# Sparse attention and token mixing on one core: value loads behind the product that frees their place, second pair's keys on ACT's queue, one turned tile, later tables, another spread of the decoding

## The chip, the cores and the metric

The kernel runs as one program on one core of a Trainium2 chip. The metric is the device time of the whole program in microseconds, from the program's start to its end; lower is better.

## The reference

Block-sparse attention over 4 batches x 8 heads x 768 positions x 64, followed by a token and channel mixer. Cut to what matters:

```
q, k, v: (4, 8, 768, 64) f32; 24 blocks of 32 positions; sampled_blocks: (24, 3) int64
mask[block i, block j] = |i-j| <= 1, or i or j in {0, 23}, or j in sampled_blocks[i]
attn = softmax(where(mask, q k^T / 8, -1e9));  x = (attn v) as (4, 768, 512)
theta = x @ w_theta;  zr, zi = x cos(theta), x sin(theta)
u = x + w_tok_r zr + w_tok_i zi   (over positions);  out = u + relu(u @ w_ch)
```

The four `moe` weights reach the device as 64-bit words, and the kernel decodes them into a high and a low part.

## The kernel before

**Units.** Two batches at a time form a pair `bp` (0 or 1). In each pair the program first does 8 *wide* units (`b`, `e`, `z`: query blocks 0 and 23 against all 768 keys), then 22 *sparse* units, one for each query block `i` from 1 to 22: that block of 32 queries for 16 heads against 8 key blocks (three of the window, block 0, block 23 and three sampled ones). All 60 units stand in the list `units`, so number 8 is the first sparse unit of the first pair and 30 the first wide one of the second.

**The order.** `tc.manual_schedule()` keeps the instructions of each engine in the order in which `attention` writes them: nothing is reordered there. The main loop is a software pipeline over steps `n`. TensorE (PE) does in step `n` the scores `S` of unit n+1, turns (transposes) the weights of unit n, and multiplies the turned weights of unit n-1 with the values into `X`. VectorE (DVE) normalises `X` of unit n-2 into `xo` (`finish`), gathers the sampled keys of unit n+2 into `kg`, takes the row extremum `m` of unit n+1's scores, and does some decoding of weights. ScalarE (ACT) copies the other keys into `kg`, does its part of the decoding, copies the turned weights from PSUM to SBUF, and takes the exponentials `P` of unit n+1. GpSimd (POOL) issues one indirect DMA per sparse unit, which gathers the values of the sampled blocks into `vb` (three buffers). After the attention the token mixer follows, whose order the framework's scheduler chooses; some of its first loads and transposes lie among the last sparse units.

**Loads.** All other DMAs are issued from SyncE's queue (SP), in the order of the program: a DMA that must wait holds back what stands behind it. `load_window` brings the window's values into `va`, of which there are two (`vas[i % 2]`), so that the load for a unit can start only when the product `X` two units earlier has read its buffer. In step n the loop writes first `finish` (with the store of `xo` to `xs`), then `load_window` of unit n and `gather_v` of unit n+1. The DMAs of queues in hardware share eight completion semaphores in turn, so each also waits until the DMA eight before it has landed. The keys `kb` of a pair have one buffer; those of the second pair are loaded on SP, with the first two value tiles `vw` of its wide units, three steps before the pair changes.

**Decoding.** The weights come in pieces of 128 x 512. Each piece takes three phases (`bits`, `rest`, `low`) on DVE, with `start` and `high` on ACT, and 66 phases cover 22 pieces. Before, a wide step does two phases and a sparse step one until none is left, so the last of the 60 units have none. After `low` of a piece SP loads the piece after next into `raw` (two buffers).

**Tables.** `Tables` loads `sampled_blocks` and makes, with some two dozen small DVE instructions, the block numbers and row numbers for the gathers. Before, it stands ahead of the first wide unit.

**Turning.** `transposed` turns up to four 128 x 128 pieces into a PSUM tile `T` (two buffers of one bank each); a sparse unit has two such tiles, `Ta` and `Tb`, each with a copy of 128 x 512 on ACT into `pa` and `pb`.

## Time and profile before

| | |
|---|---|
| time, median of 3 runs | 663.11 us (658.08 to 669.28) |
| the profiled execution | 654.65 us, of it 652.9 us span |
| mean granted TensorE clock | 0.952 |
| busy share of the span | PE 86%, DVE 71%, ACT 55%, POOL 7% |
| wide units of the first pair end near | 46 us |
| sparse units, first pair | 46 to 168 us |
| wide units of the second pair | 164 to 204 us |
| sparse units, second pair | 204 to 310 us |
| token mixer | from 288 us (first loads) to the end |

The profile is of one execution. Its rows name an engine, a line of the kernel, `out<-in`, and in brackets the idle time before an instruction with what ended it; `SPq` is the issue of a DMA on SP's queue, not the transfer. A table by stretches gives, for each stretch in us from the span's start, its length, each engine's busy time with the number of instructions, the granted clock, the share of time that the 16 DMA engines are busy, and their rate.

### The profile page before, as it was taken

The page shows a single profiled execution, that of the slowest core. Times are in us where ns is not written, and L with a number is a line of the kernel's source. Part 1 is how long each engine was busy: PE and PEld are TensorE (multiplying, and loading weights), DVE is VectorE, ACT ScalarE, POOL GpSimd, SP SyncE. Part 2 cuts the span into 40 slices and gives each one's busy share as a digit, 9 for nine tenths or more (in the row PEclk, how much of TensorE's full clock was granted, in tenths as well). Part 3 has the DMA queues.
Part 4 walks back from the last instruction along what each step waited for, and adds up shares of the span by engine and source line. Part 5 has one row for each costly group of instructions (what it writes and reads, how often), then busy time and mean ns, then how long its engine had stood idle before and what let it go on. Part 6 is the DMA issues. An engine that isn't in the chain of part 4 may idle for free.

```text
span 652.9 us, 19231 instructions
## 1 busy us (share of the span) xinstructions
PE 563.3 (86%) x7808; PEld 482.2 (74%) x7808; DVE 465.5 (71%) x1239; ACT 362.2 (55%) x834; POOL 43.5 (7%) x56
## 2 busy tenths in 40 slices
PE   4967777773977877867989999999999999999997
PEld 1545555552544655546889999999999999999997
DVE  4497798781799877845898988575783856846654
ACT  1576776771487766755656655345553456433530
POOL 1101121210100222210000000000000000000000
PEclk9997898896799988995999999999999999999999
DMA  8757889899479897776542233221142111221102
GB/s 305 229 163 201 236 247 261 237 261 326 130 233 234 231 241 215 209 208 168 144 136 81 61 83 115 93 69 49 46 134 88 63 50 43 69 67 60 33 1 96
DMA packets 79960, 96.53 MB, mean 148 GB/s; under 512 B 5312, under 2 KB 64832, under 8 KB 79488
## 3 DMA queue, kind: packets, MB, share of 16 engines
q1 hardware_dynamic: 74944, 77.73, 40.1%
q0 software_dynamic: 4928, 17.57, 10.2%
q8 instruction: 61, 1.00, 0.7%
q14 instruction: 27, 0.22, 0.1%
HBM read 82.70 MB, written 12.58 MB: 146 GB/s over the span
## 4 chain that ended last, share of the span: by engine, by line
PE 57%; DMA 22%; DVE 12%; ACT 3%; issue 3%; SPq 2%; DVEq 1%; ACTq 0%
DMA va<-in_vr_dram 14%; PE y L560 8%; PE y L561 8%; PE y L562 8%; PE X L316 5%; PE S L285 4%; PE o L583 3%; PE o L584 3%; PE o L585 3%; DMA raw_ch<-in_w_ch_dram 3%; PE h L524 3%; PE h L523 2%; PE h L522 2%; DMA xr<-xs 2%; PE Ta L303 2%
## 5 line engine op out<-in xcount | busy, mean ns | idle before, releaser
L316 PE MATMUL X<-va,pa 128*32 128x65 f32 (+1 forms) x1408 | 50.8, 239 | 45.1 <-DMA va<-in_vr_dram 41.5
L297 ACT ACTIVATE P<-S,m 128x256 f32<-128x256 f32 x176 | 69.0, 477 | 22.5 <-DVE m L288 22.4
L316 PEld LDWEIGHTS X<-va,pa 128*32 128x32 f32 (+1 forms) x1408 | 36.4, 119 | 54.8 <-DMA va<-in_vr_dram 31.9
L560 PE MATMUL y<-w_tok_r_hi,zh 128*128 128x384 f32 x192 | 64.7, 338 | 3.9 <-ACT zh L547 3.8
L288 DVE TENSOR_REDUCE m<-S 128x2 f32<-128x512 f32 x88 | 56.6, 685 | 14.2 <-PE S L285 6.8
L561 PE MATMUL y<-w_tok_r_lo,zh 128*128 128x384 f32 x192 | 64.3, 335 | 0.0
L561 PE MATMUL y<-w_tok_i_lo,zh 128*128 128x384 f32 x192 | 64.2, 334 | 0.0
L560 PE MATMUL y<-w_tok_i_hi,zh 128*128 128x384 f32 x192 | 64.1, 334 | 0.0
L562 PE MATMUL y<-w_tok_r_hi,zl 128*128 128x384 f32 x192 | 63.3, 335 | 0.0
L285 PE MATMUL S<-kg,q 64*32 64x256 f32 x1408 | 56.0, 418 | 6.8 <-issue 4.0
L562 PE MATMUL y<-w_tok_i_hi,zl 128*128 128x384 f32 x192 | 61.0, 334 | 0.0
L267 POOL DMA_INDIRECT vb<-in_vr_dram,rows x44 | 42.0, 955 | 246.5 <-PE X L316 232.6
L522 PE MATMUL h<-w_theta_hi,xTh 128*128 128x256 f32 x192 | 54.6, 285 | 0.1
L524 PE MATMUL h<-w_theta_hi,xTl 128*128 128x256 f32 x192 | 54.5, 284 | 0.0
L523 PE MATMUL h<-w_theta_lo,xTh 128*128 128x256 f32 x192 | 54.4, 283 | 0.0
L316 PE MATMUL X<-vb,pb 128*32 128x65 f32 (+1 forms) x1408 | 50.4, 237 | 0.2 <-issue 0.2
L303 PEld LDWEIGHTS Ta<-ident,P 128*128 128x128 f32 x176 | 21.3, 149 | 35.9 <-ACT P L297 22.5
L311 ACT COPY pa<-Ta 128x512 f32<-128x512 f32 x44 | 26.1, 592 | 36.4 <-PE Ta L303 36.2
L533 ACT ACTIVATE cs<-rr 128x256 f32<-128x256 f32 x48 | 19.8, 415 | 47.4 <-DVE rr L531 47.4
L303 PE MATMUL Ta<-ident,P 128*128 128x128 f32 x176 | 37.3, 314 | 9.4 <-ACT P L297 6.1
L526 ACT ACTIVATE t<-h,up_int 128x256 f32<-128x256 f32 x48 | 22.6, 472 | 39.2 <-PE h L524 32.8
L583 PE MATMUL o<-uh,w_ch_hi 128*128 128x384 f32 x128 | 42.5, 336 | 1.1 <-DVE of L589 0.9
(128 smaller groups left out, 1413.8 us busy)
## 6 DMA issues: line engine op xcount, KB each, us to landing
xa<-xs SPq DMA_DIRECT2D x192, 64.0 KB
va<-in_vr_dram SPq DMA_DIRECT2D x30, 260.0 KB
vw<-in_vr_dram SPq DMA_DIRECT2D x8, 780.0 KB
xr<-xs SPq DMA_DIRECT2D x24, 256.0 KB
out_dram<-of SPq DMA_DIRECT2D x32, 192.0 KB
q<-in_qT_dram SPq DMA_DIRECT2D x22, 256.0 KB
xs<-xo SPq DMA_DIRECT2D x44, 128.0 KB
kb<-in_kT_dram SPq DMA_DIRECT2D x3, 1536.0 KB
```

The source lines that it names most:

```text
L285: nc.tensor.matmul(sc[32 * p : 32 * p + 32, e, b, :], q[rows, b, p, :], kg[rows, :, 4 * b + p, :], start=True, stop=True)
L288: nc.vector.tensor_reduce(m[:, e], sc[:, e], axis=AX.X, op=ALU.min)
L297: nc.scalar.activation(pt[:, e, b, :], sc[:, e, b, :], AF.Exp, bias=m[:, e, b : b + 1], scale=-1.0)
L303: nc.tensor.transpose(t[:, k, :], pt, ident)
L316: nc.tensor.matmul(x[32 * p : 32 * p + 32, g, :], pt[0:rows, k, 32 * p : 32 * p + 32], v[0:rows, v0 + 65 * p : v0 + 65 * p + 65], start=st ...
L522: nc.tensor.matmul(ps, hi[:, c, :], wh[:, c, :], start=c == 0, stop=False)
L523: nc.tensor.matmul(ps, hi[:, c, :], wl[:, c, :], start=False, stop=False)
L524: nc.tensor.matmul(ps, lo[:, c, :], wh[:, c, :], start=False, stop=c == 3)
L560: nc.tensor.matmul(acc, zh[:, dd], wh[:, j, tt], start=j == 0 and m == 0, stop=False)
L561: nc.tensor.matmul(acc, zh[:, dd], wl[:, j, tt], start=False, stop=False)
L562: nc.tensor.matmul(acc, zl[:, dd], wh[:, j, tt], start=False, stop=j == 5 and m == 1)
L583: nc.tensor.matmul(ps, wh[:, c, :], uh, start=c == 0, stop=False)
```

## The change

Six things, all inside `attention`, `Tables` and the loop:

1. `load_window` moves from the start of step n (unit n, behind `finish`) to the end of the step before it (unit n+1, right behind `values` of unit n-1, the product that reads its buffer last). `gather_v` moves in the same way, to unit n+2.
2. In the second pair `kb` (two loads) and the first two `vw` are issued from ACT's queue, after the exponentials of step 27.
3. A unit's turned weights have one tile: `T` of two banks with one buffer instead of two of one bank, filled by eight (wide: six) transposes, and one copy of 128 x 1024 (768) instead of two.
4. The decoding does one phase in each step, two in the odd steps of wide units, up to one step past the last unit. It is still 66 phases.
5. `Tables` only loads at the start (its load ahead of the keys now); its DVE work, `make`, stands behind step 0.
6. The two first loads of `q` and their exclusion in the loop are written in another way; the loads are the same.

```diff
             load_edges(0)
+            tab = Tables(nc, cp, sampled)
             turn_edges(0)
             for p in range(0, 4, 2):
                 load_k(0, 0, p, 2)
-            tab = Tables(nc, cp, sampled)
...
             for n in range(len(units) + 2):
                 phases = 0
-                if 2 <= n < len(units):
-                    phases = 2 if units[n][1] == "w" else 1
+                if 2 <= n <= len(units):
+                    phases = 1 + (n < len(units) and units[n][1] == "w" and n % 2)
                 do(n - 2, finish, finish_wide)
-                do(n, load_window)
-                do(n + 1, gather_v)
...
-                    for b in range(2):
-                        load_k(1, b)
-                        load_v_wide(1, 0, b)
                 decoder.ahead(phases)
                 do(n + 1, scores, scores_wide)
                 do(n, turn, turn_wide)
                 do(n + 1, weights, weights_wide)
+                if turns:
+                    for b in range(2):
+                        load_k(1, b, queue=nc.scalar)
+                        load_v_wide(1, 0, b, nc.scalar)
                 decoder.go(phases)
+                if n == 0:
+                    tab.make(nc, cp)
                 do(n - 1, values, values_wide)
+                do(n + 1, load_window)
+                do(n + 2, gather_v)
...
-        ps_t = ctx.enter_context(tc.tile_pool(name="ps_t", bufs=2, space=PSUM))
+        ps_t = ctx.enter_context(tc.tile_pool(name="ps_t", bufs=1, space=PSUM))
...
-        def transposed(pts, name):
-            t = ps_t.tile([P, 4, 128], F32, tag="T", name=f"T{name}")
+        def turned(pts, name):
+            n = len(pts)
+            t = ps_t.tile([P, 8, 128], F32, tag="T", name=f"T{name}")
             for k, pt in enumerate(pts):
                 nc.tensor.transpose(t[:, k, :], pt, ident)
-            return t[:, : len(pts)]
+            out = wp.tile([P, 8, 128], F32, tag="pT", name=f"pT{name}")
+            nc.scalar.copy(out[:, :n], t[:, :n])
+            return out
```

On SP's queue, in the middle of the first pair's sparse units, the order before is this (`xo_7` is the result of sparse unit i = 7; the load behind it is for i = 9):

```order
L339 DMA xs<-xo_7_1447 128x2x128
L260 DMA va_119<-in_vr_dram 64x1040
L200 DMA q_13_1452<-in_qT_dram 128x512
L59 DMA raw_tok_r_1508<-in_w_tok_r_dram 128x1024
L339 DMA xs<-xo_8_1546 128x2x128
L260 DMA va_118<-in_vr_dram 64x1040
L339 DMA xs<-xo_9_1642 128x2x128
```

The same place of the changed program:

```order
L263 DMA va_119<-in_vr_dram 64x1040
L341 DMA xs<-xo_7_1388 128x2x128
L203 DMA q_13_1391<-in_qT_dram 128x512
L59 DMA raw_tok_i_1444<-in_w_tok_i_dram 128x1024
L263 DMA va_118<-in_vr_dram 64x1040
L341 DMA xs<-xo_8_1484 128x2x128
```

Each load of `va` has moved ahead of the store of the result whose product frees the buffer; in one step of three it now stands right behind a load of `raw`.

Where the pair changes, SP's queue before has the keys between two loads of values:

```order
L260 DMA va_118<-in_vr_dram 32x1040 x2
L206 DMA kb_2528<-in_kT_dram 128x3072
L346 DMA vw_0_0_2530<-in_vr_dram 128x6x260
L206 DMA kb_2528<-in_kT_dram 128x3072
L346 DMA vw_0_1_2533<-in_vr_dram 128x6x260
L339 DMA xs<-xo_19_2613 128x2x128
L260 DMA va_119<-in_vr_dram 64x1040
```

In the changed program they stand on ACT, between the exponentials of sparse unit i = 21 and the copy of its turned weights:

```order
L300 ACTIVATE P_21_2465<-S_21_2434,m_21_2451 128x256 x4
L209 DMA kb_2470<-in_kT_dram 128x3072
L348 DMA vw_0_0_2472<-in_vr_dram 128x6x260
L209 DMA kb_2470<-in_kT_dram 128x3072
L348 DMA vw_0_1_2475<-in_vr_dram 128x6x260
L80 CAST w_tok_i_hi<-da_tok_i_2345 128x512
L309 COPY pT_21_2551<-T_21_2542 128x1024
```

The four transfers have left SP's queue, and an issuing ACT stands ahead of the next copy and exponentials.

On DVE, among the first pair's wide units, two phases stand between the extrema `mw` of one unit and the next before:

```order
L357 TENSOR_REDUCE mw_011_286<-SW_011_277 128x1
L67 TENSOR_SCALAR da_theta_275<-da_theta_275 128x512
L68 TENSOR_SCALAR da_theta_275<-da_theta_275 128x512
L69 SCALAR_TENSOR_TENSOR da_theta_275<-raw_theta_183,da_theta_275 128x512
L75 TENSOR_SCALAR ds_theta_305<-da_theta_275 128x512
L77 SCALAR_TENSOR_TENSOR raw_theta_183<-raw_theta_183,ds_theta_305 128x512
L357 TENSOR_REDUCE mw_100_346<-SW_100_337 128x1
```

and one now:

```order
L359 TENSOR_REDUCE mw_011_280<-SW_011_271 128x1
L67 TENSOR_SCALAR da_theta_269<-da_theta_269 128x512
L68 TENSOR_SCALAR da_theta_269<-da_theta_269 128x512
L69 SCALAR_TENSOR_TENSOR da_theta_269<-raw_theta_143,da_theta_269 128x512
L359 TENSOR_REDUCE mw_100_332<-SW_100_323 128x1
```

In every second wide step the phase `rest`, `low` or `bits` that stood there has moved to a later step; at the far end the last seven phases now lie among the last sparse units of the second pair and one step behind them.

## The prediction

> **What bounds the kernel now.** I read the chain that ended last first, then a table by stretches, and at last the rows in order of time. In the chain the first line is by engine, the second by line:

> ```profile
> PE 57%; DMA 22%; DVE 12%; ACT 3%; issue 3%; SPq 2%; DVEq 1%; ACTq 0%
> DMA va<-in_vr_dram 14%; PE y L560 8%; PE y L561 8%; PE y L562 8%; PE X L316 5%; PE S L285 4%; PE o L583 3%; PE o L584 3%; PE o L585 3%; DMA raw_ch<-in_w_ch_dram 3%; PE h L524 3%; PE h L523 2%; PE h L522 2%; DMA xr<-xs 2%; PE Ta L303 2%
> ```

> The loads of `va` are 14% of the chain, some 90 us; the PE lines `y`, `o`, `h` are the token mixer. Then by stretches: start, wide units, sparse units in their steady part, change of pair, wide units, sparse units, tail, mixer. The columns are the stretch, its length, busy us and instructions of PE, PE's weight loads, DVE, ACT and POOL, the granted clock, the DMA engines' busy share and GB/s:

> ```profile
> 0.00:14.50 14.50, 7.25 (x32) 1.72 (x32) 5.13 (x32) 1.49 (x2) 1.46 (x12) 1.00 0.84 299
> 14.50:46.00 31.50, 25.54 (x512) 14.98 (x512) 22.01 (x42) 19.75 (x37) 2.92 (x3) 1.00 0.70 206
> 62.50:145.60 83.10, 63.70 (x1876) 44.58 (x1876) 70.06 (x186) 62.90 (x145) 17.46 (x18) 0.94 0.90 249
> 145.60:168.00 22.40, 11.60 (x174) 6.65 (x174) 5.90 (x14) 4.40 (x10) 0.00 (x0) 0.61 0.78 266
> 168.00:204.00 36.00, 30.26 (x700) 18.11 (x698) 33.55 (x69) 26.41 (x53) 2.86 (x3) 0.96 0.71 205
> 204.00:288.00 84.00, 64.17 (x1871) 44.33 (x1871) 66.44 (x182) 60.85 (x142) 16.94 (x18) 0.94 0.82 224
> 288.00:313.00 25.00, 18.06 (x357) 15.40 (x354) 13.43 (x46) 13.30 (x29) 0.91 (x1) 0.73 0.72 183
> 313.00:653.00 340.00, 331.31 (x2066) 329.33 (x2064) 235.89 (x643) 162.36 (x397) 0.00 (x0) 1.00 0.25 75
> ```

> The mixer keeps PE 97% busy and is not touched. POOL's 18 gathers count the sparse units of a steady part: 83.10 / 18 = 4.62 us a unit in the first pair and 84.00 / 18 = 4.67 in the second, of which DVE is busy 3.89 and 3.69, PE 3.5, ACT 3.5, and the DMA engines 90% and 82%. So no engine fills a unit. The wide units from 168 to 204 are another matter: DVE is 93% busy. The change of pair, 22.4 us, is idle on all engines for more than half.

> **The loop of a sparse unit**, from the rows in order of time (start, length, engine, what; in brackets the idle time before):

> ```profile
> 89.11 1.11 SPq L260 DMA_DIRECT2D va<-in_vr_dram  x1
> 90.64 0.32 PE L316 MATMUL X<-vb,pb 128*32 128x65 f32 x8
> 91.34 0.69 DVE L84 TENSOR_TENSOR w_tok_r_lo<-da_tok_r,raw_tok_r 128x512 fp32r<-128x512 f32 x1
> 92.35 0.42 DVE L326 TENSOR_TENSOR xo<-X,sm 128x256 f32<-128x256 f32 x1
> 92.53 0.35 SPq L59 DMA_DIRECT2D raw_tok_r<-in_w_tok_r_dram  x1
> 93.46 0.54 SPq L260 DMA_DIRECT2D va<-in_vr_dram  x1
> 94.67 0.32 PE L316 MATMUL X<-va,pa 128*32 128x65 f32 x8 [1.48 <-DMA va<-in_vr_dram]
> 95.49 0.30 PE L316 MATMUL X<-vb,pb 128*32 128x65 f32 x8
> 97.65 1.85 SPq L260 DMA_DIRECT2D va<-in_vr_dram  x2
> 100.33 0.32 PE L316 MATMUL X<-va,pa 128*32 128x65 f32 x8 [2.50 <-DMA va<-in_vr_dram]
> ```

> A product ends at 90.96 and frees its buffer. The next load into it is issued only at 93.46: DVE does decoding first, then `xo`, and SP stands at the store of `xo` until then. The load is used at 100.33, 6.87 us after its issue; the one of 89.11 at 94.67, after 5.56. The product at 94.67 ends at 95.79, and the load that it frees goes out at 97.65, 1.86 us later. So two units take 1.1 (product) + 1.9 to 2.5 (to the issue) + some 6.2 (to the use) = 9.2 to 9.8; the measured 2 x 4.62 = 9.24 is this loop.

> **The change, part by part.**

> *Loads of values earlier.* In two steps of three the load now waits for the product alone: 0.1 to 0.2 us instead of 1.9. In the third it stands behind a load of `raw`, which waits for DVE's L84: that ends at 92.03 here, 1.07 us after the product, and the issue takes 0.35, so 1.4 instead of 2.5. The loop becomes 1.1 + 0.2 + 6.2 = 7.5, or 8.7 with `raw`: 3.8 to 4.4 us a unit. What is late next is DVE, 3.89 busy in an order that never packs it fully, and the DMA engines: at 90% busy they can give 10%, 4.16 a unit. Bounds: no gain if those engines are saturated already, 0.73 us a unit if DVE at 3.89 set the pace. With both limits near 4.1 and the `raw` steps above them I take 4.35, 0.27 us less, in both pairs: 2 x 18 x 0.27 = **-9.7 us**. The store of `xo`, now behind the load, has a unit's time before its buffer is wanted. The gathers do not move: POOL has nothing else in its queue.

> *Second pair's keys on ACT's queue.* The rows around the change of pair:

> ```profile
> 141.70 1.57 ACT L297 ACTIVATE P<-S,m 128x256 f32<-128x256 f32 x4 [0.61 <-DVE m L288]
> 141.81 0.51 SPq L206 DMA_DIRECT2D kb<-in_kT_dram  x1
> 144.15 5.35 SPq L339 DMA_DIRECT2D xs<-xo  x1
> 149.60 0.48 SPq L260 DMA_DIRECT2D va<-in_vr_dram  x1
> 151.09 2.79 PE L355 MATMUL SW<-kb,qe 64*32 64x512 f32 x16 [4.39 <-DMA kb<-in_kT_dram]
> 162.18 0.44 PE L316 MATMUL X<-va,pa 128*32 128x65 f32 x8 [6.41 <-DMA va<-in_vr_dram]
> ```

> Behind the four issues (two halves of `kb`, two `vw`) SP's next issue holds the queue 5.35 us, so `va` goes out at 149.60 and lands behind the keys at 162.1. Now `va` leaves before them and PE's wait of 6.41 goes; but the keys are issued behind the exponentials, at 143.3 instead of 141.8, and the scores on PE wait for them 1.5 us longer. ACT pays four issues of 0.5, which it has while PE waits. -6.4 + 1.5, and about 1 for bandwidth that `va` now takes from the keys: **-4 us**; between +0.5 (ACT itself held 5.35 us, the keys 1.5 later, less the old wait) and -6.4.

> *Decoding spread out.* The phases among the second pair's wide units, on DVE in order of time (rows between left out):

> ```profile
> 181.37 0.69 DVE L83 TENSOR_TENSOR da_tok_i<-da_tok_i,w_tok_i_hi 128x512 f32<-128x512 f32 x1
> 182.70 0.95 DVE L357 TENSOR_REDUCE mw<-SW 128x1 f32<-128x768 f32 x1
> 183.56 0.41 DVE L67 TENSOR_SCALAR da_tok_r<-da_tok_r 128x512 f32<-128x512 f32 x1
> 185.20 0.43 DVE L75 TENSOR_SCALAR ds_tok_r<-da_tok_r 128x512 int32<-128x512 int32 x1
> 186.27 0.15 DVE L323 TENSOR_SCALAR sm_w<-XW 128x4 f32<-128x4 f32 x1
> 195.77 1.29 DVE L288 TENSOR_REDUCE m<-S 128x2 f32<-128x512 f32 x2
> ```

> A phase costs 1.6 (`bits`, 183.56 to 185.20), 1.1 (`rest`, to 186.27) and 1.3 us (`low`, 181.37 to 182.70), 1.35 on average. From the extremum at 182.70 to that of the first sparse unit at 195.77 three steps take 4.4 each, and DVE paces them. Three phases leave steps 32, 34 and 36 (step 30's lies in the wait for the keys): 4.05 us, unless PE, 30.26 of 36 busy, some 3.4 a step, takes over early; -3.2. In the first pair's, three leave steps 2, 4 and 6, again 4.05 us; DVE is busy 22.01 us of 31.50 there, but what is idle lies mostly ahead of the first phases (4.51 below), so -3.6. Together **-6.8**, between -3 and -8.

> The seven phases come back in steps 54 to 60, 9.5 us of DVE work. Most lies in steps whose loop I have already priced at 4.35; in the tail, 288 to 313, DVE has 11.6 us free, but the mixer's transposes queue behind the last phases: **+1.5**, between 0 and +5.

> *Tables later.* At the start DVE makes the tables before the first extremum:

> ```profile
> 8.35 5.33 PE L355 MATMUL SW<-kb,qe 64*32 64x512 f32 x28 [0.29 <-DMA kb<-in_kT_dram]
> 9.46 0.28 DVE L125 CAST sb_given<-sb_raw 128x72 f32<-128x72 int32 x1 [5.54 <-DMA sb_raw<-in_sampled_dram]
> 14.54 1.81 DVE L357 TENSOR_REDUCE mw<-SW 128x1 f32<-128x768 f32 x2
> 16.57 1.51 PE L303 MATMUL Tw<-ident,PW 128*128 128x128 f32 x6 [2.88 <-ACT PW L364]
> 20.87 0.96 DVE L357 TENSOR_REDUCE mw<-SW 128x1 f32<-128x768 f32 x1 [4.51 <-PE SW L355]
> ```

> The tables take 5.1 us (9.46 to 14.54), and later DVE idles 4.51. Moved into that gap they are free, and PE's transposes need not wait 2.88 at 16.57; the scores of unit 1 end only at 13.7, with the smaller load ahead some 0.4 later. So **-2.2**, between 0 and -4.5.

> *One turned tile.* Copies now, by form (busy, mean ns of one, idle before):

> ```profile
> L311 ACT COPY pa<-Ta 128x512 f32<-128x512 f32 x44 | 26.1, 592 | 36.4 <-PE Ta L303 36.2
> L373 ACT COPY pw<-Tw 128x256 f32<-128x256 f32 x16 | 6.1, 380 | 0.0
> L297 ACT ACTIVATE P<-S,m 128x256 f32<-128x256 f32 x176 | 69.0, 477 | 22.5 <-DVE m L288 22.4
> ```

> From 380 for 256 columns and 592 for 512, 1024 cost an estimated 592 + 2 x 212 = 1016 instead of 2 x 592, which overlap by 0.1: even. But the copy starts only after all transposes: six take 1.51 above, so the second four about 1.0, of which the first copy's 0.59 ran beside; the turn ends some 0.45 later. `P` waits for DVE's `m` 22.4 us in all, which covers that: **0**; without the cover +0.45 a unit, 20 us over 44 units.

> Sum: -9.7 - 4 - 6.8 + 1.5 - 2.2 = -21.2. The profiled execution took 654.65 (1.75 around the span): 633.4 after. It lies 8.5 below the median of the runs, 663.11, and I carry that over: 641.9, **642 us**.

> [...]

> **The rivals.**

> *A, the DMA engines are the bound (0.22).* 0.90 busy at 249 GB/s speaks for it; against it stand 299 GB/s at 0.84 in the first stretch and 266 at 0.78 around the change of pair. Earlier loads then land no earlier, and the keys steal what `va` gains: both terms go, -21.2 + 13.7 = -7.5, 655.6.

> *B, the keys interleave with the values (0.12).* A sparse unit's other traffic is 4.62 us x 249 GB/s = 1.15 MB; taken in between, it delays the keys by 1.15 / 0.266 = 4.3 us, and PE waits as long for them as it did for `va`. The keys' term is 0: 645.9. [...]

> *C, slower: ACT's longer turn (0.06).* If, with DVE relieved, `P` starts at the copy's end and not at `m`, each sparse unit pays 0.45 and each wide one 0.3: 44 x 0.45 + 16 x 0.3 = 24.6, and the loads and the wide units gain nothing, since ACT's turn paces both: 24.6 - 4 - 2.2 + 1.5 = +19.9, 683. It decides as soon as ACT waits for transposes where it now waits for `m`; the 36.2 us before `pa` speak for it, 3.5 us busy of 4.62 against it.

> *D, the load stays late (part of the forecast's range).* If the load behind `raw` in one step of three paces the rest, the unit stays at 4.5: 6 us less gain, 648.

> **How the numbers follow.** The forecast with D has 0.60, A 0.22, B 0.12, C 0.06. A measurement of this kernel can tell about 2% from no change: 13.3 us, so 649.8 is the border. Of the forecast some 0.52 lies below it, of B 0.09, of A 0.04: faster 0.65. C gives slower 0.06, the rest 0.29. The range takes in A with a poorer tail, 660; downwards the sparse units at 4.15 (36 x 0.2 = 7.2 more) and the upper ends of wide units and start (3.5) give 631, a little more 629.

> **What would show it.** Loads of `va`: issue within 0.3 us of the product's end in two of three; the idle time before `X`, 1.48 and 2.50 above, gone in most units; DVE's share near 90% in the first pair's sparse units, 4.35 us apart. Keys: the product of unit i = 21 directly behind the first `SW`, without its 6.41. Wide units: 3.3 us a step, DVE idle in the even ones. Start: first `mw` at about 11. It is wrong if the units stay at 4.6 with DMA at 0.95, if `P` waits for copies, or if the mixer's first `y` moves less than the attention's end.

## The result and the profile after

The changed kernel takes **638.8 us** (median of 4 runs, 636.82 to 639.49) against 664.38 for the kernel before in runs beside it: ratio 0.964, 95% interval 0.957 to 0.972, faster. The forecast was 642.0, range 629 to 660. The total was right; two of its terms were not, and they are of more use than the total. Stretches below are those of one execution of each kernel; how far they move from one execution to another is shown further down.

The profiled execution took 636.82 us, its span is 635.0 (before 654.65 and 652.9). The chain that ended last, first by engine, then the head of its line by lines:

```profile
PE 66%; DMA 18%; DVE 8%; issue 4%; ACT 2%; SPq 1%; DVEq 1%; ACTq 0%
PE y L555 10%; PE y L556 10%; PE y L557 10%; DMA va<-in_vr_dram 10%; PE X L318 4%; PE S L288 4%; PE T L307 4%; PE h L519 3%; PE h L518 3%; PE o L578 3%; PE h L517 3%; PE o L580 3%; PE o L579 3%; DMA kb<-in_kT_dram 3%; PE SW L357 2%
```

`va` fell from 14% to 10%; "issue", time in which an engine waits for nothing that the profile shows, rose from 3% to 4%. By stretches (columns as in the prediction): first wide units, the 18 sparse units from X of the second to X of the twentieth, change of pair, wide units, 16 sparse units of the second pair. A DMA packet's whole time counts in the stretch in which it begins, so the share of a short stretch can come out above 1:

```profile
13.00:41.50 28.50, 27.17 (x480) 14.59 (x472) 23.06 (x61) 17.74 (x27) 2.93 (x3) 1.00 0.80 256
57.70:139.30 81.60, 64.93 (x1873) 44.00 (x1872) 69.00 (x185) 61.23 (x124) 18.89 (x18) 0.96 0.93 256
139.30:151.40 12.10, 8.38 (x175) 5.67 (x174) 5.94 (x14) 4.85 (x8) 0.00 (x0) 0.86 1.04 342
151.40:187.20 35.80, 30.19 (x699) 18.11 (x698) 29.68 (x64) 25.58 (x43) 2.74 (x3) 0.95 0.76 233
196.50:273.20 76.70, 59.15 (x1664) 41.17 (x1664) 60.91 (x165) 53.64 (x111) 15.38 (x16) 0.91 0.86 230
```

The same events timed in both traces (the first row of the named tile) split the 17.8 us of span:

| stretch | before | after | difference | forecast |
|---|---|---|---|---|
| start to first sparse `m` (tables, wide units) | 46.18 | 41.48 | -4.7 | -2.2 - 3.6 |
| first sparse `m` to second `X` | 16.32 | 16.18 | -0.1 | 0 |
| first pair's sparse units, 18 | 83.09 | 81.66 | -1.4 | -4.9 |
| change of pair (`X` of i = 20 to i = 22) | 22.67 | 12.09 | **-10.6** | -4 |
| wide units, to second pair's third `X` | 46.94 | 45.09 | -1.9 | -3.2 |
| second pair's sparse units, 16 | 73.18 | 76.71 | **+3.5** | -4.9, for 18 |
| last units to the mixer's 100th `y` row | 52.11 | 50.78 | -1.3 | +1.5 |
| rest of the mixer | 312.37 | 311.05 | -1.3 | 0 |

**The loads do go out as forecast**, and yet the sparse units gained nothing. From the rows in order of time, a step of the changed kernel:

```profile
91.78 0.30 PE L318 MATMUL X<-vb,pT 128*32 128x65 f32 x8
92.02 0.79 SPq L263 DMA_DIRECT2D va<-in_vr_dram  x2
92.55 0.42 DVE L328 TENSOR_TENSOR xo<-X,sm 128x256 f32<-128x256 f32 x1
93.00 0.39 SPq L341 DMA_DIRECT2D xs<-xo  x1
```

The product ends at 92.08 and `va` is on its way at once, ahead of `xo` and its store. But one unit earlier stands this:

```profile
83.25 1.05 PE L288 MATMUL S<-kg,q 64*32 64x256 f32 x21
84.64 0.35 SPq L59 DMA_DIRECT2D raw_tok_i<-in_w_tok_i_dram  x1
88.05 1.09 PE L288 MATMUL S<-kg,q 64*32 64x256 f32 x11 [3.75 <-issue]
```

In the middle of 32 matmuls of one group PE stops for 3.75 us with nothing to wait for that the profile shows. Who waited for whom on PE between 50 and 310 us (total us, times, longest; other rows left out):

```profile
PE X L318 <- DMA va<-in_vr_dram: 18.1, 14, 3.5
PE S L288 <- issue: 10.0, 4, 4.0
PE X L318 <- issue: 8.6, 12, 1.2
PE T L307 <- ACT P L300: 5.7, 2, 4.8
PE T L307 <- issue: 4.1, 1, 4.1
```

and before:

```profile
PE X L316 <- DMA va<-in_vr_dram: 41.5, 22, 6.4
PE S L285 <- issue: 4.0, 2, 2.9
PE X L316 <- issue: 3.6, 4, 1.3
PE Ta L303 <- issue: 2.5, 1, 2.5
```

The waits for `va` lost 23 us, 6.4 of them at the change of pair; "issue" gained 12.6.

**What the pauses are.** The trace also has the DMAs that bring instructions. The page counts them as `q8 instruction`:

```profile
PE 563.2 (89%) x7808; PEld 483.1 (76%) x7808; DVE 463.5 (73%) x1239; ACT 361.0 (57%) x774; POOL 45.6 (7%) x56
q8 instruction: 61, 1.00, 0.7%
```

61 fetches of 16 KB for 2 x 7808 = 15,616 matmuls and weight loads are 256 each (PE's 153 semaphore and drain instructions not counted): I take queue 8 to feed PE, and the ends of its pauses bear that out. The longest pauses of the changed kernel beside the fetch that lies at their end, from the trace's DMA records (us):

```
PE idle from .. to     length   fetch from .. to   idle ends behind it
 84.30 ..  88.05        3.75     85.35 ..  86.53    1.52
113.49 .. 115.15        1.66    112.66 .. 113.78    1.37
233.64 .. 237.66        4.02    234.91 .. 236.11    1.55
262.81 .. 266.94        4.13    264.02 .. 265.24    1.70
```

In the 14 kernels profiled here PE has 87 such pauses of 0.8 us or more before 300 us; 85 of them end 1.21 to 1.75 us behind the end of a fetch. Fetches come every 6.1 us, so chance would put some 9% there.

A count settles it. Over all records of PE and its weight loads, the semaphore and drain instructions with them, PE stops in each of the 85 pauses at the same place: 449 instructions beyond 256 for every fetch that has come. I read this as PE having run out of instructions. In the changed kernel's mixer, where the DMA engines are busy 0.23 of the time (320 to 630 us), a fetch begins when PE is 154 to 163 beyond that mark, some 290 instructions earlier. In the sparse units it begins later: on average 4.4 us after PE has passed 154 in the changed kernel, 3.3 in the kernel before, 2.1 in the one without loads of values (told below), against 0.35 in the changed kernel's mixer. In the three longest pauses of the changed kernel PE stands 1.05 to 1.27 us before the fetch begins, and the DMA engines are at 1.03 to 1.08 in that time. The pauses of 0.8 us or more sum to 10.0 us before and 19.5 after.

### The profile page after: what moved, and what is told of

Same layout as the page of the kernel before. It is cut to its first block, busy times and chain, and to the rows that moved or that the text cites. A ratio compares the mean times of both kernels' runs of the same rounds, so it can differ in the third digit from the quotient of the medians.

```text
span 635.0 us, 19148 instructions
## 1 busy us (share of the span) xinstructions
PE 563.2 (89%) x7808; PEld 483.1 (76%) x7808; DVE 463.5 (73%) x1239; ACT 361.0 (57%) x774; POOL 45.6 (7%) x56
## 4 chain that ended last, share of the span: by engine, by line
PE 66%; DMA 18%; DVE 8%; issue 4%; ACT 2%; SPq 1%; DVEq 1%; ACTq 0%
PE y L555 10%; PE y L556 10%; PE y L557 10%; DMA va<-in_vr_dram 10%; PE X L318 4%; PE S L288 4%; PE T L307 4%; PE h L519 3%; PE h L518 3%; PE o L578 3%; PE h L517 3%; PE o L580 3%; PE o L579 3%; DMA kb<-in_kT_dram 3%; PE SW L357 2%
## 5 line engine op out<-in xcount | busy, mean ns | idle before, releaser
L300 ACT ACTIVATE P<-S,m 128x256 f32<-128x256 f32 x176 | 69.0, 477 | 15.1 <-DVE m L291 14.9
L307 PEld LDWEIGHTS T<-ident,P 128*128 128x128 f32 x352 | 42.1, 150 | 38.2 <-ACT P L300 25.9
L307 PE MATMUL T<-ident,P 128*128 128x128 f32 x352 | 60.5, 304 | 11.2 <-ACT P L300 6.1
L318 PE MATMUL X<-va,pT 128*32 128x65 f32 (+1 forms) x1408 | 50.3, 233 | 21.9 <-DMA va<-in_vr_dram 18.1
L309 ACT COPY pT<-T 128x1024 f32<-128x1024 f32 x44 | 44.8, 1018 | 41.5 <-PE T L307 41.4
L288 PE MATMUL S<-kg,q 64*32 64x256 f32 x1408 | 55.1, 404 | 10.9 <-issue 10.9
L557 PE MATMUL y<-w_tok_i_hi,zl 128*128 128x384 f32 x192 | 62.7, 334 | 0.0
L270 POOL DMA_INDIRECT vb<-in_vr_dram,rows x44 | 44.1, 1002 | 229.3 <-PE X L318 206.0
L318 PEld LDWEIGHTS X<-va,pT 128*32 128x32 f32 (+1 forms) x1408 | 35.6, 116 | 31.8 <-DMA va<-in_vr_dram 17.8
L318 PE MATMUL X<-vb,pT 128*32 128x65 f32 (+1 forms) x1408 | 49.8, 232 | 5.0 <-issue 5.0
L521 ACT ACTIVATE t<-h,up_int 128x256 f32<-128x256 f32 x48 | 22.7, 473 | 42.7 <-PE h L519 42.0
```

The source lines that it names most:

```text
L288: nc.tensor.matmul(sc[32 * p : 32 * p + 32, e, b, :], q[rows, b, p, :], kg[rows, :, 4 * b + p, :], start=True, stop=True)
L300: nc.scalar.activation(pt[:, e, b, :], sc[:, e, b, :], AF.Exp, bias=m[:, e, b : b + 1], scale=-1.0)
L307: nc.tensor.transpose(t[:, k, :], pt, ident)
L318: nc.tensor.matmul(x[32 * p : 32 * p + 32, g, :], pt[0:rows, k, 32 * p : 32 * p + 32], v[0:rows, v0 + 65 * p : v0 + 65 * p + 65], start=st ...
L557: nc.tensor.matmul(acc, zl[:, dd], wh[:, j, tt], start=False, stop=j == 5 and m == 1)
```

## The experiments

My theory after the comparison: a sparse unit now costs DVE's pace plus PE's waits for its instructions, whose fetches come late when the DMA engines are busy. Rival 1: the DMA engines' throughput alone sets the unit (the prediction's A). Rival 2: DVE does. Ratios are to the kernel before in runs of the same study.

**Part 1 undone.**

```diff
                 do(n - 2, finish, finish_wide)
+                do(n, load_window)
+                do(n + 1, gather_v)
...
-                do(n + 1, load_window)
-                do(n + 2, gather_v)
```

> The changed kernel with one part undone: the loads of values and the gathers stand ahead of the step again, as before the change. My theory: in the changed kernel a sparse unit's loop is some 4.3 us, as forecast, and the time that went missing lies in three pauses of PE of some 4 us each, in which it waits for nothing but its own next instructions. Then this kernel shows units of 4.6 us with X waiting for va again (40 us in all instead of 18) and fewer or shorter pauses, and is 3 to 9 us slower than the changed kernel (642 to 648); the change of pair stays within 3 us of 12.1. The rival, that the DMA engines are the bound: units stay at 4.5, the total within 2 us of 638.8.

655.91 us, ratio 0.993 (0.988 to 0.998): the part is worth 17 us inside the changed kernel, more than forecast and more than I expected here. In the trace 4.8 come back in the first pair's sparse units, 5.2 at the change of pair (PE waits 7.71 for the keys instead of 3.71), some 5.5 in the second pair and its end. A unit takes 4.81 and 4.87 us, longer than in the kernel before; of the first pair's 4.8 us, 4.3 are PE's busy time for as many matmuls (69.2 instead of 64.9 us, at a granted clock of 0.88 instead of 0.96). The pauses shrink to 6.2 us, as expected, and the waits for `va` rise from 18.1 to 33.1. The rival "within 2 us" is out; "change of pair within 3 us" was wrong.

**Part 2 undone.**

```diff
                 if turns:
                     turn_edges(1)
+                    for b in range(2):
+                        load_k(1, b)
+                        load_v_wide(1, 0, b)
...
-                if turns:
-                    for b in range(2):
-                        load_k(1, b, queue=nc.scalar)
-                        load_v_wide(1, 0, b, nc.scalar)
```

> The changed kernel with one part undone: the second pair's keys and first wide values are issued on SP's queue again, at their old place. My theory: the 10.6 us that the change of pair got shorter come from this part, since the load of unit i = 20 or 21 stands behind those issues again: the stretch from X of i = 20 to that of i = 22 goes from 12.1 back to 18 to 22, the total to 645 to 649. The rival: the earlier loads of values did it, being ahead of the keys on either queue: 12 to 14, total within 2 us of 638.8.

648.23 us, ratio 0.981 (0.972 to 0.989): 9 us slower than the changed kernel by the medians, in the expected range. The four runs lie wide apart, from 640.83 (the profiled one) to 651.22; the two lower ones alone would give 5 us, so the size is uncertain. The change of pair goes back to 20.7 us. Its rows:

```profile
143.37 4.70 SPq L59 DMA_DIRECT2D raw_tok_i<-in_w_tok_i_dram  x1
144.19 1.49 PE L357 MATMUL SW<-kb,qe 64*32 64x512 f32 x16 [2.11 <-DMA kb<-in_kT_dram]
148.16 0.53 SPq L263 DMA_DIRECT2D va<-in_vr_dram  x1
155.57 0.45 PE L318 MATMUL X<-va,pT 128*32 128x65 f32 x8 [8.87 <-DMA va<-in_vr_dram]
```

SP is held 4.70 us behind the keys, `va` leaves at 148.16, and PE waits 8.87 for it. What the part saves is such time on SP's queue: 4.70 us here, 5.35 behind the keys of the kernel before. In the changed kernel the same place reads:

```profile
134.78 0.38 ACTq L209 DMA_DIRECT2D kb<-in_kT_dram  x1
135.98 0.48 SPq L263 DMA_DIRECT2D va<-in_vr_dram  x1
136.25 1.02 ACTq L209 DMA_DIRECT2D kb<-in_kT_dram  x1
144.15 1.50 PE L357 MATMUL SW<-kb,qe 64*32 64x512 f32 x16 [3.71 <-DMA kb<-in_kT_dram]
147.48 0.44 PE L318 MATMUL X<-va,pT 128*32 128x65 f32 x8
151.41 0.32 PE L318 MATMUL X<-va,pT 128*32 128x65 f32 x8
```

`va` goes between the two halves of the keys, X waits for nothing, and `SW` takes 1.50 us where it took 2.79 in the kernel before. The granted clock over the stretch is 0.86 instead of 0.61.

**Fewer bytes: no gathers, then no loads of values.**

```diff
-            nc.gpsimd.indirect_dma_start(
+            if i <= VB_BUFS: nc.gpsimd.indirect_dma_start(
                 out=vb[0:96],
```

> The changed kernel without its gathers from the fourth sparse unit on (the products use what the first three left), so 400 KB of some 1160 KB that a sparse unit moves are left out and the DMA engines have a third of their time free. If PE's pauses are fetches of its instructions held up by busy DMA engines, they go (none above 1 us in the sparse units), X waits for va no more, and a unit comes to what DVE sets, 3.9 to 4.1. If the pauses have another cause, such as the number of PE's instructions, two or three of 4 us remain. If DVE set the pace already, units stay above 4.2.

```diff
-            for b0, n in fresh(i, i <= 2):
+            for b0, n in fresh(i, i <= 2) if i <= 4 else []:
```

> The changed kernel without the loads of values from the fifth sparse unit of each pair on (the products use what lies in the two buffers); the gathers stay. It leaves out 266 KB a unit, so the DMA engines should be at some 0.7, and X has no va to wait for. If PE's late instruction fetches come from the load on the DMA engines as a whole, they go here as they went without the gathers (19 to 3 us): at most 4 us of such pauses, units of 4.1, DVE's pace. If they come from the gathers' own queue, 8 us or more remain. If they come only from PE running units too fast for its fetches, they stay or grow, since nothing else holds PE.

The first leaves out the gathers from the fourth sparse unit of each pair on, some 400 KB of the 1160 KB that a unit moves, the second the loads of values from the fifth on, 266 KB. 619.88 and 621.18 us, one run each. The sparse stretches, the first two rows without gathers, the others without loads of values:

```profile
60.20:133.80 73.60, 66.69 (x1873) 42.80 (x1872) 67.94 (x185) 60.42 (x123) 0.00 (x0) 1.00 0.60 175
191.70:258.60 66.90, 60.08 (x1666) 38.07 (x1666) 60.82 (x166) 54.73 (x112) 0.00 (x0) 1.00 0.58 168
59.00:132.80 73.80, 66.56 (x1877) 42.62 (x1879) 68.28 (x185) 60.58 (x123) 17.15 (x18) 1.00 0.73 215
191.90:259.70 67.80, 62.66 (x1666) 39.74 (x1667) 59.15 (x162) 52.34 (x108) 14.93 (x16) 0.95 0.69 198
```

Units of 4.09 and 4.18, then 4.10 and 4.24 us, DVE 92% busy in the first pair, and pauses of 2.6 and 0 us. With a third or with a quarter of the traffic gone they go; the gathers' own queue is not what holds the fetches up, since with 18 gathers in the stretch there is no pause at all.

**Less work on DVE.** In the sparse units one of a piece's seven instructions stays:

```diff
-            (piece.bits, piece.rest, piece.low)[k % 3]()
+            if dve:
+                (piece.bits, piece.rest, piece.low)[k % 3]()
+            elif k % 3 == 2:
+                piece.nc.vector.tensor_tensor(piece.lo, piece.a, piece.hi.bitcast(F32), op=ALU.subtract)
...
-                decoder.go(phases)
+                decoder.go(phases, not 8 <= n < 29 and n < 40)
```

> The changed kernel with most of DVE's decoding left out in the sparse units (of the seven instructions for a piece of weights one stays; its loads and ACT's part stay), some 1.1 us of DVE's 3.8 us a unit, while the DMA engines move the same bytes. If DVE sets the pace of the units that neither wait for va nor pause, units fall below 4.3. If the DMA engines do, they stay at 4.4 to 4.6 with more waiting for va. If PE's pauses come from its instructions' fetches being late in the busy DMA queues, they stay, 6 to 20 us in all, each ending 1.3 to 1.8 us behind the end of a fetch.

645.96 us, one run, its mixer not comparable (it runs on other weights). Sparse stretches:

```profile
58.20:135.40 77.20, 64.27 (x1873) 44.19 (x1872) 50.82 (x149) 60.06 (x123) 16.74 (x18) 0.96 0.93 262
194.10:271.10 77.00, 59.60 (x1668) 41.30 (x1672) 44.30 (x132) 52.90 (x111) 15.17 (x16) 0.91 0.84 229
```

DVE is down to 66% and 58%, a unit takes 4.29 and 4.81 us: 0.25 better in the first pair, so DVE's work has a part in the pace there, and no better in the second. The waits for `va` are 5.9 us, the pauses 27, more than the 6 to 20 expected. What DVE gave in the second pair, PE's fetches took; so rival 2 is out as the sole limit.

**Raw weights behind the values** (the prediction's case D).

```diff
             if k % 3 == 2 and k // 3 + 2 < len(self.pieces):
-                self.pieces[k // 3 + 2].load(self.pool, self.queue)
+                self.due.append(self.pieces[k // 3 + 2])
...
                 do(n + 1, load_window)
+                decoder.load()
...
```

> The changed kernel with the load of raw weights, which every third step issued ahead of the load of values, issued behind it. In the changed kernel X waits for va nearly only in every third unit, where the issue was 1.1 to 1.8 us behind the product's end instead of 0.1: 18 us in all. If that position is the cause (the prediction's rival D), these waits fall below 8 us and the total to 628 to 635. If the DMA engines are the bound, the waits move elsewhere and the total stays within 2 us of 638.8. If what PE no longer waits for va it waits for its own instructions, its pauses grow from 19 to 25 or more and the total stays too.

638.64 us, ratio 0.965 (0.956 to 0.974): the same as the changed kernel. Of PE's waits between 50 and 310 us:

```profile
PE S L292 <- issue: 16.0, 6, 5.2
PE X L322 <- issue: 9.6, 9, 2.1
PE T L311 <- ACT P L304: 8.5, 7, 5.1
PE T L311 <- issue: 6.1, 2, 5.0
PE X L322 <- DMA va<-in_vr_dram: 1.6, 2, 0.9
```

The waits for `va`, 18.1 us, are gone to 1.6, so their cause was the place behind `raw`; the waits by "issue" on these lines rise from 22.7 to 31.7 and the pauses from 19.5 to 29.4. The third answer written down is the one that came, and with it the second: the waits moved and the total stayed, as it would if the DMA engines' traffic is the limit and PE meets it now in its values and now in its instructions.

**Those loads in smaller pieces**, on top of the kernel just told of.

```diff
+        for p in range(0, P, 32):
+            queue.dma_start(self.raw[p : p + 32], src[p : p + 32])
...
-            for b0, n in fresh(i, i <= 2):
+            for b0, n in [(b0 + k, 1) for b0, n in fresh(i, i <= 2) for k in range(n)]:
```

> The kernel with the load of raw weights behind that of values, whose waits for va are all gone and whose pauses of PE for its own instructions sum to 29 us, with those two loads in smaller pieces: raw in four loads of 32 partitions, the values block by block (32 rows). The bytes are the same. If a fetch waits for its turn behind one whole load on its DMA engine (eight rows of 4 KB at 234 ns are 1.9 us for raw, four of 4160 B at 232 ns are 0.9 us for va), quarter and half pieces let it in sooner: pauses below 15 us, the total 622 to 632. If it waits because the DMA engines as a whole have more queued than they move, nothing changes: pauses 20 to 30, the total 636 to 641. If SP's three issues more a unit (some 0.4 each) come to matter, waits for va return and it is 642 or more.

654.41 us, ratio 0.988 (0.983 to 0.993), 16 us slower:

```profile
57.00:145.20 88.20, 69.03 (x1872) 46.55 (x1872) 68.78 (x185) 60.11 (x124) 18.27 (x18) 0.90 0.95 230
```

The pauses are 20.9 us, less than the 29.4 of the kernel that it changes but no less than in the changed kernel, and the waits for `va` are back at 18.7: the third answer written down. The DMA engines show busier for the same bytes, 0.95 of 4.90 us a unit instead of 0.92 of 4.67. The length of single loads is not shown to hold a fetch up; by what rule it waits stays open.

**A block copied by POOL**, first ahead of the gather, then behind it.

```diff
-            for b0, n in fresh(i, i <= 2):
+            runs = fresh(i, True)
+            if i > 2:
+                kept = slice(32 * (i % 3), 32 * (i % 3) + 32)
+                nc.gpsimd.tensor_copy(va[kept], vas[(i - 1) % 2][kept])
+                runs = [(i + 1, 1)]
+            for b0, n in runs:
```

> The changed kernel with a sparse unit's middle block of values copied by POOL from the other buffer, where the unit before has it in the same partitions, instead of loaded a second time: 130 KB of some 1160 KB a unit less to move, the same result. If the DMA engines are the bound, a unit falls by 11%, from 4.54 to 4.0, the total to about 620. If the pauses for instructions are what is left, they get rarer or shorter and the total falls by 4 to 12, to 627 to 635. If DVE sets the pace, nothing is gained, and it gets slower (640 to 650) where POOL's copies hold up DVE's or the products wait for them.

> POOL copies a sparse unit's middle block of values again, as in the last run of the first study, but the gather of the next unit but one stands ahead of the copy in POOL's queue, not behind it. There the DMA engines were at 0.67 and PE waited for POOL; DVE's rows got 0.42 us a unit longer (76.6 busy instead of 69.0 in the first pair). If the queue's order was all that was wrong, a unit comes to 4.1 to 4.2 and the total to 618 to 626. If DVE, slowed by POOL's copies, sets the pace, units stay at 4.5 or above and the total at 635 to 645, with PE hardly waiting for POOL.

662.85 us, ratio 1.002 (0.998 to 1.007), and 675.42 in one run, both slower than any answer written down. The pauses do go (2.0 and 1.3 us), with the DMA engines at 0.67 in the first pair. But POOL's own waits in the second kernel are these:

```profile
POOL vb L275 <- PE X L323: 73.6, 8, 32.8
POOL va L264 <- DMA vb<-in_vr_dram,rows: 65.1, 15, 7.8
POOL va L264 <- issue: 52.6, 9, 7.5
```

The copies stand up to 7.8 us, 65 us in all, where the profile names the landing of a gather, and X waits 44 us for them. DVE's work of the 18 units grows from 69.0 to 73.1 us, and to 76.6 in the first order. A cheaper route for these 130 KB a unit was not found.

**Part 4 undone** (two phases in each wide step, one in a sparse one).

```diff
-                if 2 <= n <= len(units):
-                    phases = 1 + (n < len(units) and units[n][1] == "w" and n % 2)
+                if 2 <= n < len(units):
+                    phases = 2 if units[n][1] == "w" else 1
```

> The changed kernel with one part undone: two phases of decoding in every wide step and one in a sparse one, none in the last seven. By the prediction's sizes the wide units cost 6.8 more and the tail 1.5 less: 644. By the two traces: the first wide stretch (third extremum to the first of a sparse unit) goes from 17.2 back to 20, the second from 26.9 to 28.9, and the second pair's sparse units, which lose DVE work at their end only, and the tail give back 0 to 3: 639 to 644. The rival, that what the wide units gain the last units pay: 638.

651.05 us, ratio 0.979 (0.970 to 0.987), 12 us slower, more than the 639 to 644 expected. The first wide stretch (fourth `mw` to the first sparse `m`) goes from 17.16 to 20.73, the 3.6 of the prediction. The rest is not DVE's work: 6.4 us in the first pair's sparse units, with pauses of 11.1 us there instead of 8.3 and a granted clock of 0.90 instead of 0.96, and a wait of 5.38 for `va` at the change of pair, in a stretch whose granted clock up to the first sparse unit is 0.77 instead of 0.94. The rival is out.

**Part 3 undone** (two tiles of four blocks, a copy each).

```diff
-        ps_t = ctx.enter_context(tc.tile_pool(name="ps_t", bufs=1, space=PSUM))
+        ps_t = ctx.enter_context(tc.tile_pool(name="ps_t", bufs=2, space=PSUM))
...
-            t = ps_t.tile([P, 8, 128], F32, tag="T", name=f"T{name}")
...
+            for c in range(0, n, 4):
+                ts.append(ps_t.tile([P, 4, 128], F32, tag="T", name=f"T{name}_{c}"))
```

> The changed kernel with one part undone: two turned tiles of four blocks, each with its copy, in place of one with a single copy. The prediction has this part at 0: total within 2 us of 638.8, ACT's two copies 0.59 each. The rival that the single copy costs something, since it starts only behind all eight transposes: faster by 0.45 us in the units where X waits for nothing else, up to 10 us. The rival that it gains: one instruction less on ACT and one wait less on PE a unit, 1 to 4 us slower when undone.

638.68 us, ratio 0.961 (0.953 to 0.970) against 0.964: nothing, as forecast. The single copy in the changed kernel:

```profile
L309 ACT COPY pT<-T 128x1024 f32<-128x1024 f32 x44 | 44.8, 1018 | 41.5 <-PE T L307 41.4
```

1018 ns, for the estimate of 1016.

Since this part measures as nothing, its trace can be read almost as a second execution of the changed kernel, and the one with part 2 undone as a third, but for the change of pair; I call these two the sisters. The same events give:

| stretch | before | changed | part 3 undone | part 2 undone |
|---|---|---|---|---|
| first pair's sparse units, 18 | 83.09 | 81.66 | 83.18 | 82.27 |
| change of pair | 22.67 | 12.09 | 15.10 | 20.69 |
| wide units, to second pair's third `X` | 46.94 | 45.09 | 43.97 | 43.57 |
| second pair's sparse units, 16 | 73.18 | 76.71 | 72.89 | 72.70 |

So single stretches move by 1 to 4 us while the total stays. At the change of pair PE waits 5.25 us for the keys here, and 5.2 to 6.7 in six others of the kernels with the keys on ACT and the loads early; the 3.71 of the changed kernel's trace is less than in any of these (with part 4 undone it is 0.85, but behind the wait of 5.38 for `va`). In the second pair, pauses of 0.8 us or more come to 1.0 and 0.8 us in the two right columns, to 10.2 in the changed kernel, and a unit takes 4.56 and 4.54 us even so:

```profile
205.20:277.90 72.70, 62.22 (x1664) 41.75 (x1664) 60.75 (x164) 53.68 (x112) 15.65 (x16) 0.88 0.95 240
```

**Part 1 alone on the kernel before.** The same lines as in the first diff, the other way, with nothing else of the change.

> The kernel before with one part of the change alone: loads of values and gathers at the end of the step. Undone alone, this part cost 17 us (5 in the first pair's sparse units, 5 in the change of pair, 6 in the second pair and its end). If the parts add up, this kernel is 15 to 18 us faster than the kernel before: ratio 0.973 to 0.978. If the part needs the others (the keys still go out on SP ahead of the load at the change of pair, and units that run faster run into PE's late fetches), it gains 0 to 8: 0.988 to 1.0.

653.94 us, ratio 0.991 (0.987 to 0.995): 6 us by the ratio, 8 by the medians. The sparse units take 83.0 and 72.6 us, as before the change (83.1 and 73.2): the waits for `va` fall from 41.5 to 23.6, the pauses rise from 10.0 to 20.7. The change of pair stays at 22.45, PE waiting 6.56 for the load behind the keys.

The sparse units in one table (share and us a unit of the 18 and 16 units; waits and pauses of the whole time up to 310 us, pauses those of 0.8 us or more by "issue"; without loads of values 1.5 of the 10.0 lie in these units):

| kernel | DMA share | us a unit | waits for va | pauses |
|---|---|---|---|---|
| before | 0.90, 0.80 | 4.62, 4.57 | 41.5 | 10.0 |
| before, loads earlier | 0.94, 0.84 | 4.61, 4.54 | 23.6 | 20.7 |
| changed | 0.93, 0.86 | 4.54, 4.79 | 18.1 | 19.5 |
| changed, keys on SP | 0.94, 0.95 | 4.57, 4.54 | 30.9 | 12.5 |
| changed, two turned tiles | 0.92, 0.91 | 4.62, 4.56 | 19.7 | 12.9 |
| changed, raw behind values | 0.92, 0.84 | 4.67, 4.87 | 1.6 | 29.4 |
| changed, less decoding | 0.93, 0.84 | 4.29, 4.81 | 5.9 | 27.2 |
| changed, no loads of values | 0.73, 0.69 | 4.10, 4.24 | 10.0 | 0 |
| changed, no gathers | 0.60, 0.58 | 4.09, 4.18 | 8.8 | 2.6 |

## Why the prediction was right in the sum and wrong in two terms

- **Loads of values, -9.7: mis-sized.** The step that failed is "with both limits near 4.1 and the `raw` steps above them I take 4.35". The loop was read rightly: the loads go out at the product's end in two steps of three, `raw` delays the third (case D, shown by moving it), and DVE's pace is 4.09 (where the traffic is less). The sparse stretches gave -1.4 and +3.5 instead, and close to 0 in the two sister kernels. A limit is missing from the list: PE's instruction fetches, which in the first pair's sparse units, with the DMA engines at 0.93, begin on average 4.4 us after PE has passed 154 instructions beyond 256 for every fetch that has come, against 0.35 in the mixer at 0.23. Each of the changed kernel's three longest pauses makes a unit of 8.1 to 9.0 us. But the pauses are not the whole of what is missing: taken off, 3.75 and 8.15 us in the two stretches, they would leave 4.33 and 4.28 us a unit, while the second pair of the sisters, all but free of them, still took 4.54 and 4.56, with 8 to 10 us of waits for `va`.

  So the limit from the DMA engines, which I put at 4.16 from a share of 0.90, was not within reach: the share rose to 0.93 and the unit stayed at 4.54, close to the sign of being wrong that I had named (4.6 at 0.95). (D's 6 us are 36 x 0.15 = 5.4.) Rival A's outcome came in the sparse units. Its mechanism, the DMA engines as the bound, came in this form: PE waits now for its values, now for its instructions, and moving the one wait brought the other. How much of it is throughput and how much the place of a fetch among other transfers is not separated by these runs.
- **Keys on ACT's queue, -4: too small.** The change of pair gave -10.6 in the changed kernel's trace, -7.6 in its sister's with two turned tiles. PE's wait of 6.41 is gone in both. In the first the wait for the keys is 3.71 instead of 4.39, where I had added 1.5 to it, and PE's busy time in the stretch fell from 11.87 to 8.38 us for as many matmuls; the issues left ACT at 134.78 to 137.8, the first 4.5 us ahead of the product of i = 20, where I had reckoned with 2.3. In the sister the wait is 5.25, so part of the price of 1.5 was paid, and -10.6 is partly that execution's luck.

  What fails in "-6.4 + 1.5, and about 1 for bandwidth" is the 1 for bandwidth, of which nothing shows, and a term that is not there, the clock: granted at 0.86 over the changed kernel's stretch, at 0.61 before. PE was also less idle before than I wrote, busy 11.60 of 22.40 us. Rival B, interleaving that takes the term to 0, is out; B's picture was right (`va` does go between the keys), its price was not.
- **Decoding spread out, -6.8:** the first wide units gave 3.6 of 3.6 (shown by undoing it); the second only 1.9 of 3.2 in this trace, and in the two sisters 3.0 and 3.4. What held it back here is not DVE's work but its input: SP stands at the stores of `xo` from 144.07 for 11.4 us, the next raw weights leave at 157.34, and DVE waits 1.62 us for the first step on them. That this is what the sisters did not pay is not shown; with the keys on SP the same stores stand 16.12 us.

```profile
144.07 11.40 SPq L341 DMA_DIRECT2D xs<-xo  x3
157.34 0.35 SPq L59 DMA_DIRECT2D raw_tok_r<-in_w_tok_r_dram  x1
163.85 0.66 ACT L63 ACTIVATE da_tok_r<-raw_tok_r 128x512 f32<-128x512 f32 x1 [2.68 <-DMA raw_tok_r<-in_w_tok_r_dram]
164.54 0.43 DVE L67 TENSOR_SCALAR da_tok_r<-da_tok_r 128x512 f32<-128x512 f32 x1 [1.62 <-ACT da_tok_r L63]
```

- **Tail, +1.5:** -1.3 up to the mixer's 100th `y`, outside the bounds of 0 to +5 and of the other sign; where the last phases were paid is not shown.
- **Tables later, -2.2:** the first `mw` starts 1.4 earlier, at 13.1, not at about 11. It was not run alone.
- **One turned tile, 0:** shown. **C** did not come: `P` still waits for `m`, 14.9 us, and the one instruction of `P`'s engine that comes later, the copy, waits for the transposes as it did (41.5 us, for the 36.4 of `pa` before).

Against the sum of -21.2 for the profiled execution stand -17.8: the 34 sparse units of the two stretches fell 11 us short, the start and the second wide units 1 each, the change of pair gave 6.6 more, the tail and mixer 4 more. And the 8.5 us by which the median lay above the profiled execution did not carry over; afterwards they are 2.0. So 633.4 came out as 636.8 and 642 as 638.8: that the errors of the terms cancel is luck, and the total is closer than its terms deserve.

The parts do not add: undone one at a time they cost 17, 5 to 9, 12 and 0 us, together more than the 25.6 that the change brings, and part 1 alone gives 6 to 8. One reading is that each keeps PE from an idle time that costs more than itself, in clock (0.61 and 0.86 at the change of pair) and in what the next loads collide with; it was not tested apart.

## What to carry to other kernels

A wait that goes away pays only down to the next limit, and the limits to list are not the engines alone: where PE runs many small matmuls beside busy DMA engines, its own instructions come by DMA too (here in 61 fetches of 16 KB, with pauses of 10.0 us in all before and 19.5 after), so look for "issue" time in the middle of runs of matmuls and set the instruction fetches beside it. Take the price of a stall with the clock around it (before, 0.50 for 20.48 us, from 0.65 us ahead of the end of a wait of 4.39 us). A big transfer should not be issued on the queue from which the next small load must leave (here SP was held 5.35 and 4.70 us behind the keys). And where two executions of nearly the same kernel differ by 3 or 4 us in a stretch, one trace does not size a part to 1 us.
